# The first 128 queries of batch 0 mixed by selection matmuls instead of gathers

## The chip, the cores and the metric

One core of a Trainium2 chip runs the kernel. The metric is the device time of one execution in microseconds (us).

## The reference

Talking-heads attention, followed by a feed-forward layer with a squared ReLU. There are 8 batches, 12 heads, 448 tokens and a head width of 64; the feed-forward layer has 768 inputs, 2048 hidden units and 768 outputs.

```python
scores = scale * np.matmul(q, k.transpose(0, 1, 3, 2))
scores = np.einsum('bhij,hg->bgij', scores, w_pre)      # heads mixed before the softmax
attn = softmax(scores)                                  # over j
attn = np.einsum('bhij,hg->bgij', attn, w_post)         # heads mixed after it
x = np.matmul(attn, v)                                  # tokens x 768
h = np.maximum(x @ w_in, 0.0)
return h * h @ w_out
```

## The kernel before

The order of the instructions on PE and POOL is written out by hand; the other engines follow the order that the framework makes of the program. Each engine works through its list in order and waits on semaphores.

**Transposes.** `turn_unit` (L182, L186) transposes four heads of q and k of a batch on PE (`tr_ps`); ACT and DVE copy the results into `qT` and `kT`. For batch 0 the loads of q and k come first, in thirds, on POOL's DMA queue.

**Scores.** `score_pair` (L329, L333) computes the scores of two heads for 128 queries into two PSUM banks (`s_ps`). ACT copies one bank and DVE the other into a score block `S`, which has the queries on its 128 partitions and the heads along the free dimension. Six pairs fill a block; there are three block buffers. The next block may go into a buffer only when the readers of the old one have finished.

**Gathers.** The mix over heads is a matmul whose contracted dimension has to hold the heads. `gather` (L357) therefore copies the scores of 10 queries and 12 heads by DMA from `S` into a tile `G` with 120 rows (105 KB), in two halves of 60 rows, mostly on SP's queue. There are 8 such tiles, and 6 more at first, which lie in the last weight buffer (`w2_3`, shown as `w`) until the weights need it.

**Mix.** One turn of the main loop (`ds`, 180 turns) takes two query tiles of 10 queries. `mix` (L367) multiplies both with the 60x60 matrix `pre`, a block pattern of `w_pre`, in four matmuls of 64x64; the result is in two PSUM banks (`m_ps`). ACT takes the exponential and the row sums (L372), DVE the reciprocal (`rc`, L374), and POOL multiplies and subtracts the mean (`d`, L376).

**Unmix.** Two turns later `unmix` (L399) multiplies `d` with `post` into `at_ps`, and DVE copies that (L404) into the attention buffer `at`. `av_unit` (L199, L210) multiplies `at` with v, a third of a batch at a time. `ffn1_unit` (L251, L258, L260) and `ffn2_unit` (L281) are cut into small pieces and used as filler between turns.

**Loads.** Loads of the weights, of v and of later batches are put on POOL's queue at fixed turns (`at_load`). A load stands in line with POOL's arithmetic, so it is issued only when POOL gets there.

**Spins.** `spin` (L429) issues 16 matmuls on the identity whose results nobody uses, once before the loop and in each of turns 0 to 9.

PSUM has eight banks, which all of `tr_ps`, `s_ps`, `m_ps`, `at_ps`, `ot_ps`, `h_ps`, `o_ps` and the spins take in rotation.

Of the kernel before, what the change touches and what calls it, by code (L numbers as in the profile page):

```python
# [9 lines left out]
BF16 = mybir.dt.bfloat16  # L10
F32 = mybir.dt.float32
ACT = mybir.ActivationFunctionType
ALU = mybir.AluOpType
PE, POOL = mybir.EngineType.PE, mybir.EngineType.Pool

B, H, S, D = 8, 12, 448, 64
# [7 lines left out]
IQ = 10  # L24
# [7 lines left out]
AHEAD = 6  # L32
LEAD = 14
MORE = 6
HEAD = 3 * (AHEAD + 2 + MORE)
OFF = 64 - H * (IQ // 2)
SCALE = 1.0 / 8.0
FIRST_TURN = (13, 14, 15)
# [6 lines left out]
def kernel(  # L45
# [46 lines left out]
    def wcol(w, name, eng, p0s):  # L92
# [4 lines left out]
            eng.dma_start(out=t[p0:p0 + HR, 0:H], in_=src)  # L97
        return t

    col_pre = wcol(w_pre, "col_pre", nc.sync, (OFF, 64))  # L100
    col_post = wcol(w_post, "col_post", nc.scalar, (0, 64))

# [25 lines left out]
    for t in dts:  # L128
        nc.vector.memset(t[:, S:DW], 0.0)

    shared = wts.tile([P, FT // 4 * DMODEL], BF16, name="w2_3", tag="w2_3", bufs=1)
    gts = [work.tile([P, S], BF16, name=f"G{x}") for x in range(AHEAD + 2)]
    more = [shared[:, S * x:S * x + S] for x in range(MORE)]
    for t in gts + more:
        nc.vector.memset(t[0:OFF, :], 0.0)

    def gather_tile(n):
        if n < HEAD:
            n = n % (AHEAD + 2 + MORE)
            return more[n - AHEAD - 2] if n >= AHEAD + 2 else gts[n]  # L140
        return gts[(n - HEAD) % (AHEAD + 2)]

    def gather_end(ds):
        return min(2 * ds + AHEAD + 2 + MORE, max(HEAD + AHEAD + 2, 2 * ds + AHEAD + 2))

    attn = [atp.tile([P, VS, H, TW], BF16, name=f"at{x}") for x in range(2)]
    for t in attn:
# [3 lines left out]
    cgblk = consts.tile([P, NPAIR], F32, name="cgblk")  # L151
    wpost_bf = consts.tile([H, H], BF16, name="wpost_bf")
    w1 = [wts.tile([P, NPAIR, DFF // 4], BF16, name=f"w1_{x}") for x in range(4)]
    w2 = [wts.tile([P, FT // 4, DMODEL], BF16, name=f"w2_{x}") for x in range(3)]

    qTs, kTs, bvecs, xts, h2ts, ats = {}, {}, {}, {}, {}, {}

# [30 lines left out]
    def av_unit(b, part, cp):  # L188
        at = ats[(b, part)]
        first = part == 0  # L190
        q0 = IQ * PARTS[b % 2][part]
        n = min(IQ * PARTS[b % 2][part + 1], S) - q0
        c0 = 0 if first else 2
        ps = bank("ot_ps")
        for y in range(3):
            for r in range(VS):
                for hh in range(2):
                    g = 6 * cp + 2 * y + hh
                    nc.tensor.matmul(ps[64 * hh:64 * hh + 64, TW * y + c0:TW * y + 2 + n], lhsT=vs[b][:, g, r, :],  # L199
                                     rhs=at[:, r, g, c0:2 + n], start=(y == 0 and r == 0), stop=(r == VS - 1),  # L200
                                     skip_group_check=True)
        if b not in xts:
            xts[b] = ffnp.tile([P, NPAIR, S], BF16, name="xt", tag="xt", bufs=2)
            bvecs[b] = [work.tile([P, 3], F32, name="bvec", tag="bvec", bufs=4) for _ in range(2)]
        bv = bvecs[b][cp]
        if first:
            nc.vector.tensor_tensor(out=bv[:, :], in0=ps[:, 0:3 * TW].rearrange("p (y t) -> p y t", t=TW)[:, :, 1],
                                    in1=cgblk[:, 3 * cp:3 * cp + 3], op=ALU.mult)
        for y in range(3):
            nc.scalar.activation(out=xts[b][:, 3 * cp + y, q0:q0 + n], in_=ps[:, TW * y + 2:TW * y + 2 + n],  # L210
                                 func=ACT.Identity, bias=bv[:, y:y + 1], scale=1.0)
# [24 lines left out]
    def load_w2(x):  # L236
        n = DFF // 8
        c = x % 2 * 2
        if x == 6:
            last = wts.tile([P, FT // 4 * DMODEL], BF16, name="w2_3", tag="w2_3", bufs=1)  # L240
            w2.append(last[:, :].rearrange("p (c m) -> p c m", m=DMODEL))
        nc.gpsimd.dma_start(out=w2[x // 2][:, c:c + 2, :],
                            in_=moe_w_out[n * x:n * x + n, :].rearrange("(c p) m -> p c m", p=P))

# [87 lines left out]
        for hh, copy in enumerate((nc.scalar.copy, nc.vector.tensor_copy)):  # L332
            copy(out=Sb[n][z0:z1, 2 * p + hh, :], in_=pss[hh][z0:z1, 0:S])  # L333

    def queries(t, y):
        return max(0, min(HQ, S - IQ * t - HQ * y))

    def span_of(s):
        b, t = s
        c = IQ * t  # L340
        return half_of(b, c) // 2, half_of(b, min(c + IQ, S) - 1) // 2

    def needs(s):
# [1 line left out]

    def gather(k):

        b, t = steps[k]
        c, end = IQ * t, min(IQ * t + IQ, S)
        g = gather_tile(k)  # L350
        eng = nc.scalar if k in (1, 3) else nc.sync
        row = OFF
        while c < end:
            n, z = divmod(half_of(b, c), 2)
            x = PR * z + c % PR
            m = min(end - c, P - x)
            eng.dma_start(out=g[row:row + H * m, :], in_=Sb[n][x:x + m, :, :])  # L357
            c, row = c + m, row + H * m
        Gs[k] = g

    def mix(k):
        pss = [bank("m_ps") for _ in range(2)]
        gs = [Gs.pop(2 * k + x) for x in range(2)]
        for y in range(2):
            for x in range(2):
                rows = slice(64 * y, 64 * y + H * queries(steps[2 * k + x][1], y) if y else 64)
                nc.tensor.matmul(pss[y][64 * x:64 * x + 64, 0:S], lhsT=pre[rows, :], rhs=gs[x][rows, :],  # L367
                                 start=True, stop=True)
        for y in range(2):
            e = work.tile([P, S], F32, name="e_sb", tag="E", bufs=3)  # L370
            sm = work.tile([P, 1], F32, name="sm", tag="sm", bufs=4)
            nc.scalar.activation(out=e[:, :], in_=pss[y][:, 0:S], func=ACT.Exp, scale=SCALE, accum_out=sm[:, 0:1])  # L372
            rc = work.tile([P, 1], F32, name="rc", tag="rc", bufs=4)
            nc.vector.reciprocal(out=rc[:, :], in_=sm[:, :])  # L374
            d = dts[(2 * k + y) % ND]
            nc.gpsimd.tensor_scalar(out=d[:, 0:S], in0=e[:, :], scalar1=rc[:, 0:1], scalar2=-1.0 / S,  # L376
                                    op0=ALU.mult, op1=ALU.add)
            dsb[(k, y)] = d

    def place_of(s):  # L380
        b, t = s
        part = sum(t >= x for x in PARTS[b % 2]) - 1
        if (b, part) not in ats:
            ats[(b, part)] = attn[(3 * b + part) % 2]
        return ats[(b, part)], 2 + IQ * (t - PARTS[b % 2][part])

    def unmix(k):

        places = [place_of(s) for s in steps[2 * k:2 * k + 2]]
        us = [bank("at_ps") for _ in range(2)]  # L390
        for y in range(2):
            d = dsb.pop((k, y))
            for r in range(VS):
                c = HR * (VS * y + r)
                for x in range(2):
                    rows = slice(64 * x, 64 * x + HR)
                    for z in range(2):
                        j = PR * (r + (R - VS) * z) if r or not z else S
                        nc.tensor.matmul(us[x][PR * z:PR * z + PR, c:c + HR], lhsT=d[rows, j:j + PR],  # L399
                                         rhs=post[rows, :], start=True, stop=True)  # L400
        for x, (at, c) in enumerate(places):
            src = us[x][:, 0:2 * VS * HR].rearrange("p (y m i) -> p m y i", y=2, i=HQ)
            dst = at[:, :, :, c:c + IQ].rearrange("p r g (y i) -> p (r g) y i", y=2)
            nc.vector.tensor_copy(out=dst, in_=src)  # L404

# [27 lines left out]
    with tc.manual_schedule(engines={PE, POOL}):  # L433
# [9 lines left out]
        def at_load(i, f, *args):  # L443
            loads.setdefault(i, []).append(lambda: f(*args))
# [1 line left out]
        for x in range(2):  # L446
            at_load(-1, load_w1, x)
        for x in range(4):
            at_load(-1 if x < 2 else 2, load_v, 0, x)
            at_load(44 + 2 * x, load_v, 1, x)  # L450
        for x in range(2, 8):
            at_load(1 + x, load_w1, x)
        for x in range(6):
            at_load(11 + 2 * x, load_qk, 1, x)
            at_load(52 + 2 * x, load_qk, 2, x)
# [2 lines left out]
        for b in range(1, B):  # L458
            if b + 2 < B:
                for x in range(6):  # L460
                    at_load(NT * b + 34 + 2 * x, load_qk, b + 2, x)
            if b + 1 < B:
                for x in range(4):
                    at_load(NT * b + 46 + 2 * x, load_v, b + 1, x)
        nd = len(steps) // 2
        issued, gathered = [NPAIR + 3], [0]
        spans = [span_of(s) for s in steps]
# [9 lines left out]

        def scores_for(ds, most):
            want = math.ceil(place(gather_end(ds) + LEAD - 2))
            full = sum(gathered[0] >= x for x in lasts)  # L480
            want = min(want, issued[0] + most, NPAIR * min(full + 3, blocks))
            want = max(want, needs(steps[min(2 * ds + 4, len(steps) - 1)]))
            while issued[0] < want and all(issued[0] % NPAIR < turned.get(x[1], 0) for x in halves(issued[0] // NPAIR)):
# [10 lines left out]
        gathers_for(-1)  # L494
        for n in range(NPAIR, issued[0]):
            score_pair(n)
        spin(4)
        for f in loads.get(-1, []):
            f()
        for ds in range(nd + LAG):  # L500
            for i in (2 * ds, 2 * ds + 1):
                for f in loads.get(i, []):
# [19 lines left out]
            if old2:  # L522
                unmix(ds - LAG)
                for b1, t1 in old2:
                    ends = PARTS[b1 % 2]
                    if t1 + 1 in ends:
# [1 line left out]
                        for x, u in enumerate(av_units(b1, part)):  # L528
                            at_step(ds + (2 + x if b1 else 1), u)
                        if b1 == 0:  # L530
                            c = (IQ * ends[part], min(IQ * ends[part + 1], S))
                            at_step(ds + 1, (0, lambda c=c: filler.extend(ffn1_units(0, *c))))
                    if t1 == NT - 1:
                        if b1 > 0:
# [8 lines left out]
            if now2:  # L543
                mix(ds)
            gathers_for(ds)
            if ds < PARTS[0][1] // 2 + LAG:
                spin(4)
            if ds + 1 < nd + LAG:
                fill(share)
# [39 lines left out]
```

The softmax here doesn't subtract the row's maximum and nothing guards it: scores larger than these inputs give would overflow.

## Time and profile before

| What | Value |
|---|---|
| Median of 13 runs | 588.53 us (583.49 to 593.37) |
| The profiled execution | 587.95 us, with a span of 586.2 us |
| Mean granted PE clock | 0.982 |
| PE busy | 542.4 us, 93% of the span |
| DVE, ACT, POOL busy | 408.0, 407.4, 399.4 us |
| First 60 us: PE busy | 36.21 us |
| Gathers in the chain that ended last | 4% of the span for `G<-S`, 3% for `w<-S` |

The span goes from the first to the last instruction of the profiled execution. The page divides it into forty slices of 14.65 us each. Busy shares are averages over stages with different limits, so tables by stage and the chain of waits matter more than the totals. "w" in the profile stands for several weight buffers: for `w1`, for `w2`, and for the six gather tiles that lie in `w2_3`.

### The profile page before, as it was taken

How to read it: one execution, taken by the hardware profiler on the slowest of the kernel's cores; microseconds unless marked ns; L12 is line 12 of the kernel's file. 1: busy time of each engine (PE TensorE's matmuls, PEld its weight loads, DVE VectorE, ACT ScalarE, POOL GpSimd, SP SyncE). 2: the span in 40 equal slices, each digit the busy share in tenths (PEclk: the TensorE clock that was granted, in tenths of full speed). 3: DMA queues.
4: the chain of work that ended last, by engine and by line, in shares of the span. 5: the costliest groups of instructions: out<-in, count | busy, mean ns of one | idle time of the engine just before them, and what ended most of it. 6: DMA issues, size and time to landing. Idle time of an engine off the chain costs nothing.

```text
span 586.2 us, 28172 instructions
## 1 busy us (share of the span) xinstructions
PE 542.4 (93%) x11810; PEld 309.3 (53%) x11810; DVE 408.0 (70%) x1050; ACT 407.4 (70%) x1223; POOL 399.4 (68%) x599
## 2 busy tenths in 40 slices
PE   2776997999899999999999999999999999999997
PEld 1443765655455555545655556545545555555554
DVE  5767786889777787677777787778777778756001
ACT  3756786878588767896688767886688768863320
POOL 5466578847667965897678865897578666782540
PEclk9979799999899999999999999999999999999999
DMA  9899879858963698448953697459943477442103
GB/s 136 142 217 178 186 152 162 160 103 156 196 137 75 109 192 169 93 87 146 206 115 73 117 199 149 90 89 173 192 101 75 83 153 145 85 79 57 41 14 82
DMA packets 83364, 74.98 MB, mean 128 GB/s; under 512 B 6436, under 2 KB 80164, under 8 KB 83236
## 3 DMA queue, kind: packets, MB, share of 16 engines
q1 hardware_dynamic: 51502, 49.26, 36.1%
q0 software_dynamic: 31264, 23.60, 29.8%
q8 instruction: 92, 1.51, 1.0%
q10 hardware_dynamic: 470, 0.32, 0.2%
q14 instruction: 36, 0.29, 0.1%
HBM read 47.20 MB, written 11.01 MB: 99 GB/s over the span
## 4 chain that ended last, share of the span: by engine, by line
PE 78%; DMA 7%; DVE 4%; ACT 3%; POOL 2%; issue 2%; ACTq 0%; DVEq 0%
PE o_ps L281 25%; PE h_ps L251 25%; PE at_ps L399 10%; PE ot_ps L199 7%; PE m_ps L367 6%; DMA G<-S 4%; PE s_ps L329 4%; DMA w<-S 3%; DVE at L404 2%; PE tr_ps L182 2%; ACT xt L210 2%; POOL d L376 1%; ACT e_sb L372 1%; POOL w L232 1%; DVE S L333 1%
## 5 line engine op out<-in xcount | busy, mean ns | idle before, releaser
L376 POOL TENSOR_SCALAR d<-e_sb,rc 128x448 bf16<-128x448 f32 x360 | 226.6, 640 | 146.9 <-DVE rc L374 145.5
L404 DVE CAST at<-at_ps 128x480 bf16<-128x480 f32 x360 | 220.0, 651 | 67.0 <-PE at_ps L399 60.2
L372 ACT ACTIVATE e_sb<-m_ps 128x448 f32<-128x448 f32 x360 | 195.7, 559 | 21.8 <-PE m_ps L367 16.8
L251 PE MATMUL h_ps<-xt,w 128*128 128x448 bf16 (+2 forms) x960 | 164.3, 320 | 1.7 <-DVE at L404 1.3
L281 PE MATMUL o_ps<-w,h 128*128 128x384 bf16 (+1 forms) x1024 | 163.1, 329 | 0.5 <-ACT xt L210 0.5
L260 POOL TENSOR_TENSOR h<-hr 128x448 bf16<-128x448 f32 (+2 forms) x136 | 113.7, 845 | 15.9 <-ACT hr L258 15.9
L251 PEld LDWEIGHTS <-w 128*128 128x128 bf16 x960 | 80.8, 99 | 78.3 <-issue 29.3
L281 PEld LDWEIGHTS <-h 128*128 128x128 bf16 (+1 forms) x1024 | 82.4, 101 | 71.9 <-issue 26.7
L333 ACT CAST S<-s_ps 128x448 bf16<-128x448 f32 (+1 forms) x174 | 90.8, 542 | 41.5 <-PE s_ps L329 40.7
L333 DVE CAST S<-s_ps 128x448 bf16<-128x448 f32 (+1 forms) x174 | 104.5, 614 | 0.4 <-PE s_ps L329 0.4
L399 PEld LDWEIGHTS <-d 60*64 60x64 bf16 x5760 | 64.1, 110 | 58.0 <-issue 35.7
L399 PE MATMUL at_ps<-post,d 60*64 60x60 bf16 x5760 | 84.8, 195 | 9.3 <-issue 3.8
L258 ACT ACTIVATE hr<-h_ps 128x448 f32<-128x448 f32 (+2 forms) x160 | 74.5, 487 | 19.5 <-PE h_ps L251 13.7
L374 DVE RECIPROCAL rc<-sm 128x1 f32<-128x1 f32 x360 | 53.0, 158 | 44.4 <-ACT e_sb L372 42.0
L367 PE MATMUL m_ps<-G,pre 64*64 64x448 bf16 (+2 forms) x684 | 73.9, 358 | 10.5 <-DMA G<-S 6.7
L372 ACT ACTIVATION_READ_ACCUMULATOR e_sb<-m_ps 128x1 f32 x360 | 78.8, 219 | 0.0
L210 ACT ACTIVATE xt<-ot_ps,bvec 128x160 bf16<-128x160 f32 (+3 forms) x144 | 44.7, 385 | 45.4 <-PE ot_ps L199 36.1
L329 PE MATMUL s_ps<-kT,qT 64*64 64x448 bf16 x672 | 64.2, 370 | 0.8 <-issue 0.3
L288 DVE COPY osb<-o_ps 128x384 f32<-128x384 f32 x48 | 26.0, 548 | 36.8 <-PE o_ps L281 36.6
L199 PE MATMUL ot_ps<-at,v 128*64 128x160 bf16 (+4 forms) x1152 | 45.9, 229 | 0.0
L199 PEld LDWEIGHTS <-v 128*64 128x64 bf16 x1152 | 38.4, 109 | 13.7 <-issue 12.3
L367 PEld LDWEIGHTS <-pre 64*64 64x64 bf16 x720 | 28.4, 107 | 30.0 <-issue 22.4
(42 smaller groups left out, 214.6 us busy)
## 6 DMA issues: line engine op xcount, KB each, us to landing
G<-S SPq DMA_DIRECT2D x314, 105.0 KB
out_dram<-osb SPq DMA_DIRECT2D x48, 192.0 KB
v<-in_v_dram POOLq DMA_DIRECT2D x32, 192.0 KB, 5.7
qkst<-in_k_dram POOLq DMA_DIRECT2D x24, 224.0 KB, 5.5
qkst<-in_q_dram POOLq DMA_DIRECT2D x24, 224.0 KB, 6.4
w<-in_moe_w_in_dram POOLq DMA_DIRECT2D x8, 384.0 KB, 10.6
w<-in_moe_w_out_dram POOLq DMA_DIRECT2D x8, 384.0 KB, 6.3
w<-S SPq DMA_DIRECT2D x15, 105.0 KB
```

The source lines that it names most:

```text
L199: nc.tensor.matmul(ps[64 * hh:64 * hh + 64, TW * y + c0:TW * y + 2 + n], lhsT=vs[b][:, g, r, :], rhs=at[:, r, g, c0:2 + n], start=(y == 0 ...
L251: nc.tensor.matmul(ps[:, 0:n], lhsT=w1[ft // 4][:, c2, ft % 4 * 128:ft % 4 * 128 + 128], rhs=xts[b][:, c2, c0:c1], start=(c2 == 0), stop=( ...
L258: nc.scalar.activation(out=hr[:, 0:n], in_=ps[:, 0:n], func=ACT.Relu)
L260: square.tensor_tensor(out=h2ts[(b, ft)][:, c0:c1], in0=hr[:, 0:n], in1=hr[:, 0:n], op=ALU.mult)
L281: nc.tensor.matmul(dst, lhsT=h2ts[(b, ft)][:, mt * 128:mt * 128 + ROWS[mt]], rhs=w2[ft // 4][:, ft % 4, n2 * 384:(n2 + 1) * 384], start=(f ...
L329: nc.tensor.matmul(pss[hh][PR * z:PR * z + PR, 0:S], lhsT=qTs[b][rs, p, PR * j:PR * j + PR], rhs=kTs[b][rs, p, :], start=True, stop=True)
L333: copy(out=Sb[n][z0:z1, 2 * p + hh, :], in_=pss[hh][z0:z1, 0:S])
L367: nc.tensor.matmul(pss[y][64 * x:64 * x + 64, 0:S], lhsT=pre[rows, :], rhs=gs[x][rows, :], start=True, stop=True)
L372: nc.scalar.activation(out=e[:, :], in_=pss[y][:, 0:S], func=ACT.Exp, scale=SCALE, accum_out=sm[:, 0:1])
L376: nc.gpsimd.tensor_scalar(out=d[:, 0:S], in0=e[:, :], scalar1=rc[:, 0:1], scalar2=-1.0 / S, op0=ALU.mult, op1=ALU.add)
L399: nc.tensor.matmul(us[x][PR * z:PR * z + PR, c:c + HR], lhsT=d[rows, j:j + PR], rhs=post[rows, :], start=True, stop=True)
L404: nc.vector.tensor_copy(out=dst, in_=src)
```

## The change

Thirteen tiles (`FIRST`) now cover the first 128 queries of batch 0, which are exactly score block 0. For these tiles there is no gather. Instead, `mix` multiplies the score block itself with weighted selection matrices. For each head h and each half of 64 queries, `zs` holds, for every query, a column for each output head with the weight `w_pre[h, g]` in the row of that query. Sixty-four such columns starting at the tile's first query, multiplied with the score block of head h and accumulated over the twelve heads, give the mixed scores of five queries. This is 48 matmuls of 64x64 for two tiles instead of four.

The matrices are built at the start from the identity and from a broadcast copy of `w_pre` (`wpre`, loaded on SP ahead of `col_pre`). DVE builds the parts for heads 0 to 7 in four products, POOL those for heads 8 to 11 in one. They lie in the buffers that later hold `w_out`. A tile now takes five queries from each half of the block, so `unmix` copies its result in two pieces. Tiles 13 to 44 of batch 0 take 10 queries each from query 128 on; the first third of batch 0 has 158 queries instead of 160.

The loads of v and `w_in` come earlier. All four loads of v of batch 0 and four of the eight of `w_in` are issued ahead of the loop and the other four at turns 0 to 3. The clearing of the six extra gather tiles moves from DVE to POOL in turns 0 to 2. The spin before the loop is gone, and the ones in the loop run in turns 6 to 9 alone. The gathers that ran on ACT's queue are gone; all gathers are on SP's queue.

```diff
+FIRST = 13
+FQ = 128
+ROUND = AHEAD + 2 + MORE
+HEAD = FIRST + 2 * ROUND
+ZH = 4
+ZW = 64 * H
...
+    wpre = shared[:, MORE * S:MORE * S + 2 * H * H].bitcast(F32)
+    nc.sync.dma_start(out=wpre,
+                      in_=bass.AP(tensor=w_pre.tensor, offset=w_pre[0, 0:1].offset, ap=[[0, P], [1, H * H]]))
...
-    for t in gts + more:
+
+    for t in gts:
         nc.vector.memset(t[0:OFF, :], 0.0)
...
+    zs = [wts.tile([P, ZH * ZW], BF16, name=f"w2_{x}", tag=f"w2_{x}", bufs=1) for x in range(3)]
+    idz = shared[:, MORE * S + 2 * H * H:MORE * S + 2 * H * H + 64]
+    nc.vector.tensor_tensor(out=idz, in0=ident[:, 0:64], in1=ident[:, 64:P], op=ALU.add)
+
+    def z_unit(x, eng, h0=0, h1=ZH):
+        eng.tensor_tensor(out=zs[x][:, ZW * h0:ZW * h1].rearrange("p (h q g) -> p h q g", h=h1 - h0, g=H),
+                          in0=idz.unsqueeze(1).unsqueeze(3).to_broadcast([P, h1 - h0, 64, H]),
+                          in1=wpre.rearrange("p (h g) -> p h g", g=H)[:, ZH * x + h0:ZH * x + h1, :].unsqueeze(2).to_broadcast([P, h1 - h0, 64, H]),
+                          op=ALU.mult)
+
+    for x in range(2):
+        for h in range(0, ZH, 2):
+            z_unit(x, nc.vector, h, h + 2)
...
     def gather(k):
 
+        if by_pe(k):
+            return
...
-        eng = nc.scalar if k in (1, 3) else nc.sync
+        eng = nc.sync
...
     def mix(k):
         pss = [bank("m_ps") for _ in range(2)]
-        gs = [Gs.pop(2 * k + x) for x in range(2)]
+        pair = (2 * k, 2 * k + 1)
+        gs = [None if by_pe(n) else Gs.pop(n) for n in pair]
+        for h in range(H):
+            for y in range(2):
+                rows = slice(64 * y, 64 * y + 64)
+                for x, n in enumerate(pair):
+                    if by_pe(n):
+                        c = ZW * (h % ZH) + H * query(0, n)
+                        m = min(64, ZH * ZW - c)
+                        nc.tensor.matmul(pss[y][64 * x:64 * x + m, 0:S], lhsT=zs[h // ZH][rows, c:c + m],
+                                         rhs=Sb[0][rows, h, :], start=(h == 0), stop=(h == H - 1),
+                                         skip_group_check=True)
...
+            if by_pe(2 * k + x):
+                for y in range(2):
+                    j = c + FQ // 2 * y
+                    nc.vector.tensor_copy(out=at[:, :, :, j:j + HQ].rearrange("p r g i -> p (r g) i"), in_=src[:, :, y, :])
+                continue
...
         for x in range(4):
-            at_load(-1 if x < 2 else 2, load_v, 0, x)
+            at_load(-2, load_v, 0, x)
             at_load(44 + 2 * x, load_v, 1, x)
         for x in range(2, 8):
-            at_load(1 + x, load_w1, x)
+            at_load(-2 if x < 4 else 2 * x - 8, load_w1, x)
...
+        for f in loads.get(-1, []):
+            f()
+        z_unit(2, nc.gpsimd)
+        for f in loads.get(-2, []):
+            f()
+        for x, t in enumerate(more):
+            at_load(x, nc.gpsimd.memset, t[0:OFF, :], 0.0)
...
-            full = sum(gathered[0] >= x for x in lasts)
+            full = sum(gathered[0] >= x for x in lasts) if 2 * ds >= FIRST else 0
...
-        spin(4)
-        for f in loads.get(-1, []):
-            f()
...
-            if ds < PARTS[0][1] // 2 + LAG:
+            if FIRST // 2 <= ds < PARTS[0][1] // 2 + LAG:
                 spin(4)
```

## The prediction

> **What bounds the kernel now.** I read first the page's forty slices, then the chain of waits, then tables by stage and the timeline of the first 100 us, because the edit touches only the first 128 queries.
>
> ```profile
> PE   2776997999899999999999999999999999999997
> DMA  9899879858963698448953697459943477442103
> 0.00:60.00 60.00, 36.21 (x906) 22.44 (x906) 38.30 (x114) 32.63 (x89) 34.91 (x60) 0.94 1.00 171
> 200.00:250.00 50.00, 49.20 (x1159) 27.75 (x1157) 37.15 (x96) 36.36 (x111) 34.77 (x53) 1.00 0.77 147
> 17.04 3.73 DMA G<-S
> 33.03 12.32 DMA G<-S
> 47.08 11.49 DMA w<-S
> 67.60 3.33 DMA w<-S
> ```
>
> The two stage rows give length, then busy time of PE, PEld, DVE, ACT and POOL, then clock, DMA share, GB/s. From 200 us on PE is busy 49.20 of 50 us: PE sets the end, its order is fixed by the program, so a delay or gain early moves the whole rest. In the first 60 us PE is idle for 23.8 us while the DMA engines are full (share 1.00), and the chain (start, length, cause) runs through gathers for 27.5 us of it. That is what the change attacks. A gain here counts one for one, up to the moment when PE becomes full, which I put at loop turn ds=13 (two query tiles a turn); its mix ends at 62.7 us in the timeline.
>
> ```profile
> 8.28 0.62 DVE L186 COPY kT<-tr_ps 128x896 bf16<-128x896 bf16 x1 [0.18 <-PE tr_ps L182]
> 14.74 3.80 DVE L333 CAST S<-s_ps 128x448 bf16<-128x448 f32 x7
> 16.98 1.78 PE L429 MATMUL spin_ps<-ident 64*64 64x448 bf16 x16
> 27.50 0.93 PE L429 MATMUL spin_ps<-ident 64*64 64x448 bf16 x16
> 20.81 0.59 PE L367 MATMUL m_ps<-G,pre 64*64 64x448 bf16 x4 [1.68 <-DMA G<-S]
> 56.38 1.25 POOL L376 TENSOR_SCALAR d<-e_sb,rc 128x448 bf16<-128x448 f32 x2
> 57.22 1.01 DVE L260 TENSOR_TENSOR h<-hr 128x160 bf16<-128x160 f32 x1
> 57.60 0.44 POOL L260 TENSOR_TENSOR h<-hr 128x160 bf16<-128x160 f32 x1
> ```
>
> Timeline rows (start, length): DVE is the first to be needed after the transposes, at 8.28, and its casts of scores decide when mixing may begin. PE's sixteen spin matmuls take 1.78 us early and 0.93 us later. DVE's 160-element product, 0.32 us at 61.45, took 1.01 us when POOL worked beside it.
>
> [...] the 1.01 us product began at 57.22, inside POOL's second d (ends 57.63), and ended at 58.23, after POOL's h (ends 58.04): it waited for both. [...] 16 matmuls in 0.93 us are a 0.36 us one plus three rounds of 0.19 us, so four run together. [...]
>
> **The change part by part.** The sum is made against the profiled run: span 586.2 us, time 587.95, so 1.75 us lie around the span. It is 0.6 below the median of 588.53; I add the difference to the median.
>
> A. *Building the selection weights.* The order of the changed program puts four DVE products of 128x1536 (zs 0 and 1) ahead of every kT copy, behind `post`, which waits for col_post until 7.87. No row shows this size; [...] They run from 8.3 to 15.2 if nothing blocks them. Behind them queue three kT copies (0.62 each) and the score casts (0.55 each); PE waits for both. By program order eleven score pairs precede mix(0), and with eight PSUM banks mix(0) needs the eighth cast: 15.2 + 3x0.62 + 8x0.55 = 21.5. Before, mix(0) was at 20.81. The gather of 3.73 us is saved, yet the start is +0.7. The w_pre broadcast on SP (74 KB) lands before 8 us and delays only col_pre, by one issue of 0.85 us, hidden by the wait for col_post. Removing six DVE memsets (1.45 us, L135) gains nothing, since DVE waits for col_post anyway.
>
> B. *The same product on POOL* (zs 2, 128x3072) becomes ready at 8.3 as well, when idz is done. POOL's h rows give (932-388)/320 = 1.70 ns an element, so 5.4 us; [...] I take 6.0. [...] Lower bound 0: DVE's four hold on one after another, POOL comes last, and mix(0) needs zs 2 only at head 8. [...] I take 6.0 for zs 2 plus 0.7 for one DMA issue: +6.7. POOL itself, with v and w1 behind zs 2, is free by about 22 and its first d is due after 26: no cost. The six memsets of 4x448 on POOL (a DVE one took 0.245) fit in the same slack, three turns at about 2.5 us of POOL work under a 2.7 us turn.
>
> C. *The mixes.* 48 matmuls for 4, in 12 rounds of 0.19: 2.4 us for 0.6, so +1.8 in turn 0. [...] I add 1.5 for half clock (bounds 0, and 2.2 when the whole mix is slow). M0, the end of mix(0), moves by 0.7+1.8+1.5 = +4.0. Turns 1 to 6 then: a turn allocates up to eight banks (two at, four scores, two m), so in turns 2 and 3 a mix must wait for the two exps of the turn before, 1.25 us: 2.7+3.6+3.6+3.0+2.8+1.8 = 17.5. Before, these six took 39.1-21.4 = 17.7. So -0.2: thirteen missing gathers are paid for in matmuls. DVE's by-half copies (four of about 0.4 for two of 0.61) give 3.1 us in those turns, under 3.6. The seven spin groups removed lay in idle PE time: 0.
>
> D. *Turns 7 to 13.* Gathers for tiles 13 to 26 start when the second score block is cast, at turn 1, and SP needs 0.88 for each issue: 14 are out 12.3 us later, before their mixes. So the DMA waits go, and DVE is late next: two rc 0.32, two copies 1.22, casts 0.61, some 0.1 between, 2.25 a turn; seven turns and one attention-times-V of 1.87 are 17.6. Before: 62.7-39.1 = 23.6. So -6.0 (bounds -3 with w1 and qk loads still crowding, -7). v and w1 issued earlier have landed by then; the qk loads, one a turn on POOL, are the new last arrival for the transposes of turn 13.
>
> E. *After turn 13.* PE is near full. Of the 3.33 us wait at 67.60 I take 0.7 as gained (0 to 3); the rest of the program is the same.
>
> Sum: +4.0 -0.2 -6.0 -0.7 = -2.9 without the exclusion of B; +6.7 with it: +3.8. On the median: 592.3.
>
> **Rivals.** *R1, no exclusion at the start* (DVE keeps its turn, or POOL's product slips behind): -2.9, 585.6, on the other side. For it: DVE's four instructions stand back to back, and the trace shows no such pair at this length. Against: 1.01 us at 57.22, where POOL's next instruction passed the waiting DVE. It decides at B: when the last zs product on DVE ends before about 18.1 us (15.2+2.9), the change wins. *R2, R1 with a larger relief*: less traffic also removes the 3.33 us wait and the PE gap at 97.13 (3.40 us, put down to "issue"): 588.5-2.9-2.6-3.4 = 579.6. For: 1.4 MB less in the full stage. Against: that gap comes 35 us later. *R3, half clock lasts*: the mixes stay slow through several turns [...]: 6.5 mixes at 4.5 instead of 2.25 us, less the 1.5 counted: +13 at most, half of it +6.5, so 598.8. For: clock 0.55 from 35 to 40 us in the trace[...].
>
> **How the numbers follow.** Forecast 0.55 (its own range 587.5 to 597), R1 0.23, R2 0.09, R3 0.13. A difference of 0.5% (2.9 us) is about what a measurement can tell from no change. Slower by more: 0.37 of the forecast's 0.55 and all of R3, 0.50. Faster: 0.03 of the forecast, half of R1 and R2 whole, 0.24. The rest, 0.26, within. The range leaves out half of R2 and the ends of R3: 582 to 598.
>
> **What would show it.** In the profile after: [...] the first kT copy near 22 us (15.2 in R1); first mix near 28, lasting 2.4 to 4.5; no DMA wait before tiles 13 to 26; mix of turn 13 ending near 67.2 (60.5 in R1). I am wrong if the four DVE products end by 16 us, or if the turns after 6 still wait for gathers.

## The result, and the profile after

The changed kernel takes 598.89 us (median of 11 runs, 594.94 to 602.34) against 587.54 (48 runs of the kernel before, made beside them). The ratio of the two is 1.0193, with a 95% interval of 1.0165 to 1.0222: 11.3 us slower. The prediction had 592.3 and a range up to 598. The profiled execution has a span of 598.9 us. Executions more than 1.5% above the fastest of their kernel are left out of the ratios below but not of the medians, and r9_spin16 was profiled in one of them, so its trace is used for positions only.

The slices of the page after (tenths of busy time, forty slices) and the row of the first stage (columns as before):

```profile
PE   1398789789999999999999999999999999999997
DMA  8878957985995389646974499548953477342103
```
```profile
0.00:60.00 60.00, 34.24 (x887) 23.23 (x891) 41.87 (x106) 24.46 (x63) 37.23 (x55) 0.97 0.83 137
```

In the first 60 us the DMA share falls from 1.00 to 0.83: the gathers of the first 13 tiles are gone. PE is nevertheless busy for 2.0 us less than before. A mix now takes 48 matmuls instead of 4, but PE gets less far in these 60 us (887 matmuls against 906). The first two slices show why (1 and 3, before 2 and 7): PE stands still at the start. The timeline of the start (start, length), with `post` of the kernel before as the first line:

```profile
7.87 0.22 DVE L118 TENSOR_TENSOR post<-stripe_post,col_post 128x60 bf16<-128x60 f32 x1 [1.27 <-DMA col_post<-in_w_post_dram]
```
```profile
11.35 0.22 DVE L127 TENSOR_TENSOR post<-stripe_post,col_post 128x60 bf16<-128x60 f32 x1 [0.63 <-DMA col_post<-in_w_post_dram]
11.70 11.95 DVE L182 TENSOR_TENSOR w<-w 128x1536 bf16<-128x1536 bf16 x4
11.76 6.94 POOL L182 TENSOR_TENSOR w<-w 128x3072 bf16<-128x3072 bf16 x1 [4.05 <-DVE w L179]
13.38 6.93 DVE L182 TENSOR_TENSOR w<-w 128x1536 bf16<-128x1536 bf16 x1
23.57 1.14 DVE L221 COPY kT<-tr_ps 128x896 bf16<-128x896 bf16 x2
29.56 2.89 PE L412 MATMUL m_ps<-S,w 64*64 64x448 bf16 x48
```

`post` waits for col_post until 11.35 (7.87 before). Then DVE's four products take 11.95 us together. One by one they take 1.76, 6.93, 1.75 and 1.75 us: the second (shown alone in the fourth line) ends at 20.31, 1.61 us after POOL's product (18.70). The kT copies and every score follow the products. The chain of waits (start, length, cause) has this start in it, and three later places:

```profile
2.36 8.86 DMA col_post<-in_w_post_dram
11.70 11.95 DVE w L182 x4
...
52.21 0.75 SPq L397
53.06 1.21 DMA G<-S
54.81 0.52 ACT S L368
...
71.98 3.38 issue
...
79.32 1.41 issue
```

To follow the delay through the program, I take from the traces the start of the second exp of a turn on ACT (us). "Control" is the changed kernel profiled once more (run r14_after_again).

| kernel | turn 0 | 6 | 13 | 16 | 40 | 179 | median |
|---|---|---|---|---|---|---|---|
| before | 21.9 | 40.2 | 63.7 | 72.0 | 138.3 | 532.9 | 587.54 |
| after | 32.8 | 50.9 | 70.8 | 85.4 | 151.9 | 545.4 | 598.89 |
| control | 33.0 | 53.9 | 70.5 | 79.8 | 146.6 | 541.7 | 597.05 |
| r5_one_head | 23.6 | 42.8 | 59.3 | 71.5 | 139.5 | 532.3 | 588.28 |
| r6_loads_before | 32.7 | 52.2 | 76.9 | 86.3 | 153.4 | 550.4 | 604.04 |
| r7_all | 25.1 | 43.6 | 60.0 | 71.7 | 141.0 | 534.9 | 589.88 |
| r10_all_w2_later | 24.3 | 43.4 | 60.5 | 69.3 | 137.9 | 532.5 | 589.33 |
| r11_all_spin8 | 24.1 | 42.6 | 59.4 | 69.5 | 137.0 | 531.5 | 589.22 |
| r13_all_spin8_w2 | 28.0 | 46.4 | 62.7 | 72.2 | 140.8 | 534.5 | 589.94 |

The rows are single executions, the medians are over the timed runs. From turn 40 to the end every row lasts 392.8 to 397.0 us (394.6 before), so what decides the kernel happens in the first quarter.

### The profile page after: what moved, and what is told of

Read it like the earlier page. It is cut to its first block, busy times and chain, and to the rows that moved or that the text cites. A ratio compares the mean times of both kernels' runs of the same rounds, so it can differ in the third digit from the quotient of the medians.

```text
span 598.9 us, 28505 instructions
## 1 busy us (share of the span) xinstructions
PE 547.3 (91%) x11984; PEld 315.3 (53%) x11984; DVE 419.4 (70%) x1062; ACT 407.2 (68%) x1223; POOL 408.5 (68%) x606
## 4 chain that ended last, share of the span: by engine, by line
PE 77%; DVE 7%; DMA 6%; ACT 5%; issue 3%; POOL 2%; ACTq 0%; SPq 0%; DVEq 0%; POOLq 0%
PE o_ps L316 24%; PE h_ps L286 23%; PE at_ps L452 9%; PE ot_ps L234 7%; PE m_ps L420 5%; PE s_ps L364 4%; DMA G<-S 3%; PE m_ps L412 3%; DVE at L462 2%; DVE w L182 2%; PE tr_ps L217 2%; ACT e_sb L425 2%; ACT xt L245 2%; DMA col_post<-in_w_post_dram 1%; POOL d L429 1%
## 5 line engine op out<-in xcount | busy, mean ns | idle before, releaser
L462 DVE CAST at<-at_ps 128x480 bf16<-128x480 f32 x347 | 212.1, 651 | 63.5 <-PE at_ps L452 55.0
L286 PE MATMUL h_ps<-xt,w 128*128 128x448 bf16 (+3 forms) x960 | 165.4, 320 | 5.8 <-issue 2.7
L295 POOL TENSOR_TENSOR h<-hr 128x448 bf16<-128x448 f32 (+3 forms) x136 | 113.6, 844 | 16.4 <-ACT hr L293 16.4
L286 PEld LDWEIGHTS <-w 128*128 128x128 bf16 x960 | 81.4, 99 | 81.8 <-issue 32.7
L452 PEld LDWEIGHTS <-d 60*64 60x64 bf16 x5760 | 64.1, 109 | 51.0 <-issue 32.5
L293 ACT ACTIVATE hr<-h_ps 128x448 f32<-128x448 f32 (+3 forms) x160 | 74.4, 485 | 20.9 <-PE h_ps L286 14.6
L420 PE MATMUL m_ps<-G,pre 60*64 60x448 bf16 (+2 forms) x670 | 73.3, 357 | 6.0 <-DMA G<-S 2.7
L245 ACT ACTIVATE xt<-ot_ps,bvec 128x160 bf16<-128x160 f32 (+5 forms) x144 | 44.7, 385 | 45.5 <-PE ot_ps L234 36.2
L234 PE MATMUL ot_ps<-at,v 128*64 128x160 bf16 (+5 forms) x1152 | 45.9, 229 | 0.0
L234 PEld LDWEIGHTS <-v 128*64 128x64 bf16 x1152 | 38.4, 109 | 13.5 <-issue 12.1
L420 PEld LDWEIGHTS <-pre 64*64 64x64 bf16 (+2 forms) x694 | 27.0, 107 | 19.0 <-issue 16.5
```

The costliest lines, as they stand in the source:

```text
L286: nc.tensor.matmul(ps[:, 0:n], lhsT=w1[ft // 4][:, c2, ft % 4 * 128:ft % 4 * 128 + 128], rhs=xts[b][:, c2, c0:c1], start=(c2 == 0), stop=( ...
L293: nc.scalar.activation(out=hr[:, 0:n], in_=ps[:, 0:n], func=ACT.Relu)
L295: square.tensor_tensor(out=h2ts[(b, ft)][:, c0:c1], in0=hr[:, 0:n], in1=hr[:, 0:n], op=ALU.mult)
```

## The experiments

The theory to be tested has three parts. The start costs about 11 us (building the matrices, and the late col_post). The relief in turns 7 to 13 is partly taken by a wait for a score block's buffer. What is left is taken by PE's idle stretches in turns 14 and 15, which the chain calls "issue". Rivals: the loads or the gathers bound these turns anyway; half clock carries the loss. With each result stands its ratio to the kernel before, run in the same group, and the 95% interval of that ratio. The kernel before had medians of 586.42 to 587.54 in these groups.

### The start: POOL's product, w_pre's place, nearly no matrices

r1_no_pool_product leaves POOL's product out:

```diff
-        z_unit(2, nc.gpsimd)
...
-lhsT=zs[h // ZH][rows, c:c + m]
+lhsT=zs[min(h // ZH, 1)][rows, c:c + m]
```

> POOL's product for heads 8 to 11 is left out; the mix reads the matrices of heads 4 to 7 again for these heads, so the values of the first 128 queries are wrong and only the time counts. Theory (the two products exclude each other): DVE's four products take 6.9 us instead of 11.95, the first kT copy and the first mix come 5 us earlier, and the end moves by about -5 us (594). Rival (the four are slow in themselves, or POOL's DMA issues hold DVE as well): they stay near 12 us and the time stays at 599.

Measured: 597.16 us, ratio 1.0165 [1.0133, 1.0197]. DVE's timeline:

```profile
11.82 6.76 DVE L182 TENSOR_TENSOR w<-w 128x1536 bf16<-128x1536 bf16 x4
18.50 1.15 DVE L221 COPY kT<-tr_ps 128x896 bf16<-128x896 bf16 x2
```

The four products take 6.76 instead of 11.95 us: POOL's one instruction costs DVE 5.19 us. The exp of turn 0 comes at 28.0, 4.8 earlier than in the changed kernel. So the mechanism of the theory is shown, but not its gain of 5 us: the median falls by 1.7 us only, and the intervals of the two ratios overlap. (The profiled execution, 594.44 us, was the fastest of the four.)

r2_wpre_behind issues the broadcast of w_pre later:

```diff
-    nc.sync.dma_start(out=wpre, ...)     # ahead of col_pre
...
     for t in gts:
         nc.vector.memset(t[0:OFF, :], 0.0)
+    nc.vector.memset(wpre, 0.0)
+    nc.sync.dma_start(out=wpre, ...)     # behind col_pre and col_post
```

> The broadcast load of w_pre goes out behind the two col_pre loads on SP instead of ahead of them; nothing else moves. Theory (128 rows of 576 bytes ahead of the small loads hold them up): col_pre and col_post land near 6.4 and 7.9 us as before the change, DVE's products start near 8.5 instead of 11.7, and the end moves by -3 us (596). Rival (the small loads are late for another reason, such as the loads of q and k): they land at 10.5 and 11.4 as now, no change; or the products now wait for w_pre itself, no change either.

Measured: 596.91 us, 1.0132 [1.0086, 1.0178]. The edit also clears wpre first, so the broadcast is issued at 3.39 us instead of 0.76. col_post is used at 7.45, but the products wait for w_pre itself until 9.96:

```profile
9.96 8.61 DVE L183 TENSOR_TENSOR w<-w 128x1536 bf16<-128x1536 bf16 x2 [2.19 <-DMA w<-in_w_pre_dram]
```

The exp of turn 0 is at 31.2, 1.6 earlier. In the profiles with the broadcast ahead of the columns `post` runs at 10.85 to 14.1; with it behind, at 6.97 to 8.77 in five of six (11.81 in r13). So the late column goes with the early broadcast. How one delays the other is not shown. col_post goes out on ACT's queue, not on SP's. The last packet of the broadcast ends at 3.55 us, that of col_post at 10.92, and in between (3.6 to 11 us) the packets of POOL's queue take 99.2% of the time of the 16 engines. Moving the broadcast is worth little alone, since the next input is late too.

r5_one_head takes the building away nearly whole:

```diff
-    for x in range(2):
-        for h in range(0, ZH, 2):
-            z_unit(x, nc.vector, h, h + 2)
+    z_unit(0, nc.vector, 0, 2)
...
-        z_unit(2, nc.gpsimd)
...
-c = ZW * (h % ZH) + H * query(0, n)
-m = min(64, ZH * ZW - c)
+c = H * query(0, n)
+m = min(64, 2 * ZW - c)
...
-lhsT=zs[h // ZH][rows, c:c + m]
+lhsT=zs[0][rows, c:c + m]
```

> The changed kernel with one product of 128x1536 on DVE in place of four, and none on POOL; every head's mix reads the matrices of the first head group, so the output of the first 128 queries is computed with the weights of the wrong heads; the instructions of the mixes, their number and their tiles stay. It takes nearly the whole of steps A and B away and leaves C, D and E. Theory (the building of the matrices sets the start, and PE is full later): the first exp falls from 32.8 us to about 23, near the 21.9 of before, and the time falls by most of these 10 us, to 588 to 591. Rival (what is gained at the start meets the gathers and loads, whose pace DMA sets, and PE's waits in turns 7 to 16 grow by as much): first exp near 23 all the same, but the time at 593 to 597, with the delay against before growing from about 1 us in turn 0 to 7 or more by turn 16.

Measured: 588.28 us, 1.0020 [0.9993, 1.0047].

```profile
11.62 1.76 DVE L182 TENSOR_TENSOR w<-w 128x1536 bf16<-128x1536 bf16 x1
...
20.31 2.89 PE L410 MATMUL m_ps<-S,w 64*64 64x448 bf16 x48
```

The time falls by 10.6 us, so the products account for the size of the loss, even though `post` is as late here (11.27) as in the changed kernel. But part of what the rival foresaw is there too: at turn 13 this kernel is 4.4 us ahead of before (59.3 against 63.7), at turn 16 only 0.5. Mixing without gathers does gain; three turns give it back. That DMA's pace takes it, as the rival had it, this run does not show.

### The loads

r6_loads_before and r8_before_loads exchange the schedules of v and w_in:

```diff
# r6, on the changed kernel
-            at_load(-2, load_v, 0, x)
+            at_load(-2 if x < 2 else 2, load_v, 0, x)
...
-            at_load(-2 if x < 4 else 2 * x - 8, load_w1, x)
+            at_load(1 + x, load_w1, x)
# r8, on the kernel before
-            at_load(-1 if x < 2 else 2, load_v, 0, x)
+            at_load(-1, load_v, 0, x)
...
-            at_load(1 + x, load_w1, x)
+            at_load(-1 if x < 4 else 2 * x - 8, load_w1, x)
```

> The changed kernel with the load schedule of before for v and w_in (two v loads and two w_in loads at the start, the others one turn after the other), all else as in the changed kernel. Theory (PE's idle stretches in turns 14 and 15 come from its instruction fetch waiting behind loads, whichever loads they are; w_out's are the ones there): they stay, 597 to 600. Rival (the loads that run on without a pause are what fills the DMA queues at the wrong time): 592 to 595, with turns 13 to 16 back near the 8.3 us of before from the 14.6 of the changed kernel.

> The kernel before with the load schedule of the changed kernel (v and the first w_in loads at the start without a pause), and its gathers as they were. Theory (the load schedule is nearly neutral; the matrices and what follows from them cost the time): 586 to 590. Rival (the loads in a row delay gathers or the instruction fetch and cost several us by themselves): 592 or more.

Measured: r6 604.04 us, 1.0267 [1.0201, 1.0334]; r8 586.48 us, 0.9974 [0.9950, 0.9998]. Both expectations of r6's time missed: the old schedule is not better but worse. (Its turns 13 to 16 took 9.4 us, near what the rival said, but the control, with no edit at all, took 9.3.) r6's timeline at turn 7:

```profile
59.69 0.95 ACT L368 CAST S<-s_ps 64x448 bf16<-64x448 f32 x2 [6.85 <-DMA w<-S]
60.27 1.71 PE L487 MATMUL spin_ps<-ident 64*64 64x448 bf16 x16 [6.70 <-ACT S L368]
```

A cast of a score waits 6.85 us for gathers, and PE behind it 6.70. SP issues the gathers at nearly the same times as in the changed kernel (from 33.8 and 33.9 us on), but with loads spread over the first turns they land later: the chain waits from 37.53 to 59.55 for them. So the part of the change that lets the loads run on does what it should; by itself it is worth 0.26% on the kernel before, with an interval that only just excludes no change.

### Turn 7: the buffer of the fourth score block

In the changed kernel the same cast waits:

```profile
54.38 0.95 ACT L368 CAST S<-s_ps 64x448 bf16<-64x448 f32 x2 [2.81 <-DMA G<-S]
54.96 0.95 PE L487 MATMUL spin_ps<-ident 64*64 64x448 bf16 x16 [2.80 <-ACT S L368]
```

The fourth score block needs one of the three score buffers. No gather reads block 0 in this kernel, and PE has mixed it by then. So a cast that waits for gathers is not going into the buffer of block 0: the pool has given it that of a block which the gathers are still reading (block 1, with its thirteen gathers, is the next oldest).

r3_slots gives every third block the same buffer:

```diff
-            Sb[n] = work.tile([P, H, S], BF16, name="S", tag="S", bufs=3)
+            Sb[n] = work.tile([P, H, S], BF16, name="S", tag=f"S{n % 3}", bufs=1)
```

> Score blocks go into three fixed buffers in turn, so the fourth block takes the place of block 0, which no gather reads, instead of block 1. Theory (the first cast of the fourth block waits for the thirteen gathers of block 1): the wait of 2.8 us of ACT at 51.4 goes, turn 8's mix comes 2.4 us earlier, the end moves by about -2.4 us (596.5). Rival (later turns are bound by the order of DVE and the transposes and give it back): less than 1 us.

Measured: 595.05 us, 1.0127 [1.0094, 1.0159], as the theory had it, and the only one of the single repairs whose interval lies below that of the changed kernel. From the exp of turn 6 to that of turn 7 it takes 2.0 us instead of 4.8, although `post` was as late as 12.68 in that profile. Without this edit the step is not always long: it took 2.0 us in r5 and 2.2 in the control.

### Everything at once

r7_all puts the repairs together: the slots of r3, w_pre behind as in r2, nothing on POOL, and the products in another form:

```diff
+    idz12, wpb = shared[:, 0:ZW], shared[:, ZW:ZW + H * H]
+    nc.vector.tensor_copy(out=idz12.rearrange("p (q g) -> p q g", g=H), in_=idz.unsqueeze(2).to_broadcast([P, 64, H]))
...
+    nc.vector.tensor_copy(out=wpb, in_=wpre)
...
+        nc.vector.tensor_tensor(out=zs[x][:, :].rearrange("p (h q g) -> p h q g", h=ZH, g=H),
+                                in0=idz12.rearrange("p (q g) -> p q g", g=H).unsqueeze(1).to_broadcast([P, ZH, 64, H]),
+                                in1=wpb.rearrange("p (h g) -> p h g", g=H)[:, ZH * x:ZH * x + ZH, :].unsqueeze(2).to_broadcast([P, ZH, 64, H]),
+                                op=ALU.mult)
```

> The changed kernel with all of the repairs at once: the three products on DVE alone in bf16 (inputs first copied to bf16, with the innermost run contiguous), none on POOL, the w_pre broadcast behind col_pre on SP, and score block n in buffer n modulo 3. Theory (A, B and the score block's slot explain most of the 11 us): the products take 1.6 to 3.2 us each and end by 16 to 21 us instead of 23.65; first exp at 24 to 29; no wait of the fourth score block for gathers in turn 7; time 588 to 592, about as before. If PE's waits for its instruction stream and for loads in turns 13 to 16 take the place of what is gained: 593 to 596.

Measured: 589.88 us, 1.0022 [0.9994, 1.0050], within what its theory had.

```profile
10.84 5.10 DVE L188 TENSOR_TENSOR w<-w 128x3072 bf16<-128x3072 bf16 x3
```

All three matrices are ready at 15.94 us, turn 7 no longer waits (2.0 us), and turn 13 comes 3.7 us ahead of before. At turn 16 the lead is 0.3. As in r5, the rest of the loss sits in turns 14 to 16.

### Turns 14 and 15: the "issue" stretches of PE

PE's timeline of the changed kernel:

```profile
69.79 0.99 PE L286 MATMUL h_ps<-xt,w 128*128 128x158 bf16 x12
...
71.56 0.42 PE L217 MATMUL tr_ps<-ident,qkst 64*64 64x64 bf16 x29
75.36 0.58 PE L217 MATMUL tr_ps<-ident,qkst 64*64 64x64 bf16 x27 [3.38 <-issue]
...
76.25 1.76 PE L286 MATMUL h_ps<-xt,w 128*128 128x158 bf16 x12
```

PE stops in the middle of 56 transposes, and the profile shows nothing that the rest of them waits for. The next h_ps group then runs at little over half speed (1.76 against 0.99 us; the granted clock from 76.0 to 78.2 us is 0.50). Counting matmuls in the trace, the stretches of 3.38, 1.41 and 2.69 us lie ahead of numbers 1245, 1373 and 2013, whole multiples of 128 apart. The trace also has packets of 16 KB on a DMA queue of their own (q8, kind "instruction"), one for about 128 matmuls with their weight loads (93 for 11984 on the page). One of them lies in or just ahead of each of these stretches: the first starts at 72.96, 0.98 us after PE has stopped, and takes 0.95 us. DMA queues of the changed kernel from 71 to 76 us (packets, MB, share of 16 engines):

```profile
q0 software_dynamic: 360, 0.52, 66.4%
q8 instruction: 1, 0.02, 1.2%
```

The traces of all runs together make this much stronger. They have 74 "issue" stretches of PE longer than 0.7 us, the first hundred matmuls left out. In every one PE goes on 1.2 to 1.8 us after the end of a 16 KB packet, and every one lies at a remainder of 82 to 95 modulo 128 (62 of them at 92 to 95; the remainder drifts down slowly through the program).

r4_w2_later moves the w_out loads, the ones under way there:

```diff
-            at_load(22 + 3 * x + (4 if x > 5 else 0), load_w2, x)
+            at_load(31 + 3 * x - (5 if x > 5 else 0), load_w2, x)
```

> The first six loads of w_out go out nine loop steps (4.5 turns) later. Theory (the PE gaps of 3.38 us at 72.0 and 1.41 us at 79.3 are instruction fetches that wait behind these loads): the gaps in turns 14 and 15 go, the end moves by -4 to -5 us (594.5). Rival (the gaps are waits for the transposes' own data, or fetches that are late at every 128th matmul whatever the loads): the gaps stay, 599; second rival: they move with the loads to later turns, 599.

Measured: 599.50 us, 1.0191 [1.0155, 1.0227]: no gain. The two stretches are still there, with 0.91 and 1.06 us. Turns 13 to 16 take 8.6 us instead of 14.6, turns 16 to 40 then 70.4 instead of 66.5: partly given back. (`post` ran at 14.1 in this profile.) As the control below shows, turns 13 to 16 can be that short without the edit.

r9_spin16, r15_spin8 and r11_all_spin8 shift the work against the count:

```diff
         for x in range(4):
             if x < 3:
                 turn_unit(0, x, (nc.scalar.copy, nc.vector.tensor_copy))
+            if x == 1:
+                spin(16)        # r15 and r11: spin(8)
```

> The changed kernel with 64 spin matmuls more, put in PE's idle 9.7 us at the start (14.5 to 24.2), where they should cost nothing. In the changed kernel PE's idle stretches of 3.38, 1.41 and 2.69 us lie ahead of the matmuls number 1245, 1373 and 2013 of the trace. These numbers are whole multiples of 128 apart, and 128 matmuls with their weight loads are one 16 KB packet of the instruction queue. Theory (PE waits for its instruction stream): the stretches stay at about the same numbers modulo 128 (1245, 1373, 2013), 64 matmuls earlier in the work, or vanish. Rival (PE waits for data or a semaphore of the work there): they move with the work to 1309, 1437 and 2077. Time 596 to 601 by both; down to 594 if the stretches vanish at the new place.

> The changed kernel with 32 spin matmuls in PE's idle 9.7 us at the start. Theory (borders of the instruction packets): an idle stretch stays at matmul 1245 and the one at 1373 shrinks below 1 us, as with the same shift in r11_all_spin8; turns 13 to 16 take 11 to 13 us instead of 14.6; 595 to 598. Rival (the shift by 64 matmuls cost time [...]): 601 or more.

> The changed kernel as it is, as a control beside the next run: 597 to 601 us, idle stretches of PE ahead of matmuls 1245 and 1373, more than 3 us together. If these stretches are not a property of the program but of one execution, they are elsewhere or absent, and their sum is below 2 us.

> r7_all with 32 spin matmuls more in PE's idle time ahead of the first scores. If the place of the instruction packets' borders in the work decides how long PE waits for them, the idle stretches of turns 14 and 15 (1.90 and 2.16 us, ahead of matmuls 1245 and 1373) stay at these numbers, 32 matmuls earlier in the work, and their lengths change; the time moves by up to 3 us either way from 589.9. If data is what PE waits for: the same stretches at 1277 and 1405, and 589 to 591.

Measured: r9 606.20 us, 1.0275 [1.0189, 1.0362]; r15 600.43 us, 1.0206 [1.0145, 1.0268]; the control r14 597.05 us, 1.0204 [1.0163, 1.0245]; r11 589.22 us, 1.0056 [1.0023, 1.0090]. PE in r15, with the work 32 matmuls later in the count:

```profile
69.64 0.72 PE L452 MATMUL at_ps<-post,d 60*64 60x60 bf16 x29
73.99 0.26 PE L452 MATMUL at_ps<-post,d 60*64 60x60 bf16 x3 [3.62 <-issue]
...
77.30 0.35 PE L217 MATMUL tr_ps<-ident,qkst 64*64 64x64 bf16 x21
79.09 0.47 PE L217 MATMUL tr_ps<-ident,qkst 64*64 64x64 bf16 x35 [1.44 <-issue]
```

The stretches stay at 1245 and 1373, and the first now cuts a group of at_ps instead of transposes. r9, with a shift of 64, has them at 1245 and 1373 too, where they cut a group of h_ps and one of at_ps; r11 has them there with 2.06 and 0.84 us. So PE waits for its instruction stream there, not for data: this is shown. What a shift is worth isn't: r15's expected gain did not come, and r9's interval is wide and reaches down to the changed kernel's. The control shows how much is the execution's own:

```profile
71.31 0.42 PE L217 MATMUL tr_ps<-ident,qkst 64*64 64x64 bf16 x29
72.48 0.41 PE L217 MATMUL tr_ps<-ident,qkst 64*64 64x64 bf16 x27 [0.76 <-issue]
...
75.94 0.22 PE L217 MATMUL tr_ps<-ident,qkst 64*64 64x64 bf16 x3 [1.06 <-issue]
```

The same two places, 0.76 and 1.06 us: below the 2 us that its rival named. Another such wait of 2.30 us had come in turn 6 (ahead of matmul 607), where r12 has one of 2.58. The place is the program's; the length changes from one execution to the next.

The lengths matter. In the fourteen profiles of the changed kernel and its variants (r9 left out), the time from turn 13 to turn 16 goes with the sum of the "issue" time of PE in it (correlation 0.91). It is 8.6 to 9.4 us where the sum is 2.0 us or less (r4, r6, the control), 13.5 and 14.6 us where it is about 5 (r15 and the changed kernel).

r10, r12 and r13 try to keep the lead on top of r7: r10 with r4's edit, r13 with r4's and r11's, r12 with each of the first six w_out loads in two halves:

```diff
-            at_load(22 + 3 * x + (4 if x > 5 else 0), load_w2, x)
+            if x > 5:
+                at_load(26 + 3 * x, load_w2, x)
+            else:
+                at_load(22 + 3 * x, load_w2, x, (0,))
+                at_load(24 + 3 * x, load_w2, x, (1,))
```

> The kernel with all repairs (run r7_all) and the first six w_out loads nine loop steps later. In r7_all turn 13 ends 3.7 us ahead of before (second exp at 60.0 against 63.7) and turn 16 level with it (71.7 against 72.0). Theory (w_out's loads make the instruction packets late in turns 14 and 15): turns 13 to 16 take 8.3 to 9 us, the lead stays, and the time is 584 to 587. Rival (the lead is given back wherever the loads are put, since the DMA engines have the same bytes to move by the first use of w_out at about 117 us): turns 13 to 16 quicker all the same, loss of 3 us or more between turns 20 and 40, time 588 to 592.

> r7_all with each of the first six w_out loads (384 KB) cut into two of 192 KB, a loop turn apart; the same bytes at nearly the same time. Theory (an instruction packet is late by the burst ahead of it): the idle stretches of turns 14 and 15, 4.06 us together, shrink to about half, time 586 to 588. Rival (it is late by the mean traffic of loads and gathers, or by a packet fetched too close ahead of its use, not by the burst): they stay within 1 us of 4, time 589 to 591.

> r7_all with both edits that shortened turns 13 to 16: 32 spin matmuls ahead of the first scores, and the first six w_out loads nine loop steps later. Theory (late instruction packets in turns 14 and 15 are what takes the lead of 3.7 us): both idle stretches gone, second exp of turn 16 at 68 to 69.5 against 72.0 in before, time 583.5 to 586. Rival (PE is not the only limit between turns 16 and 40; the lead is lost there to loads that come later): turn 16 at 68 to 69.5 all the same, 587 to 590.

Measured: r10 589.33 us, 1.0018 [0.9991, 1.0045]; r12 589.93 us, 1.0046 [1.0019, 1.0072]; r13 589.94 us, 1.0059 [1.0033, 1.0086]. In all three the rival fits the time better. r10 keeps 2.7 us of its 3.2 us lead at turn 16, and 0.4 at turn 40. r12's two stretches shrink to one of 2.30 us, but turn 6 has lost 2.58 at matmul 607. r13's start was late (`post` at 11.81, turn 0 at 28.0), so that its turn 16 is level with before; its turns 13 to 16 took 9.5 us, with stretches of 1.65 and 1.11 us still there. No version of the changed kernel beats the kernel before.

Why an instruction packet comes late in one execution and in time in another stays open. The DMA share (the number before the last) from turn 13 to turn 16 does not decide it. These are the rows of before, r7 and r10:

```profile
63.70:72.00 8.30, 7.96 (x274) 6.14 (x275) 6.76 (x18) 7.16 (x24) 6.49 (x11) 0.85 0.79 178
60.00:71.70 11.70, 7.45 (x261) 5.33 (x259) 7.44 (x19) 7.07 (x24) 7.41 (x13) 0.88 0.97 177
60.50:69.30 8.80, 6.50 (x240) 4.84 (x231) 6.75 (x18) 6.87 (x23) 5.88 (x10) 1.00 0.57 95
```

Before has no such stretch at a share of 0.79, the changed kernel 4.8 us of them at the same share, the control 1.8 at 0.91, r7 4.1 at 0.97, and r10 still 2.1 at 0.57. Neither moving nor halving the w_out loads removes the loss for good.

## Why the prediction was wrong, step by step

**A, B and C were right in sum, not in their terms.** They gave +10.7 us at the end of the first mix (4.0 plus 6.7) and +10.5 after turn 6; the traces show +10.9 (32.8 against 21.9) and +10.7. In A col_post was 3.5 us later than assumed: "delays only col_pre, by one issue of 0.85 us" is the sentence that failed. The stretch from 8.3 to 15.2 for the four products (6.9 us) was the author's estimate, on no row of before; without POOL's product they take 6.76 us (r1). B's exclusion, for which before has a single DVE product (1.01 us beside POOL, 0.32 alone), came: the second product took 6.93 us beside POOL's, the others 1.75 or 1.76. It cost 5.2 us (11.95 less 6.76), not 6.7. POOL's record is 6.94 us long, yet DVE's first product fills its beginning (to 13.46); the 5.24 us left are near the 5.4 that the prediction worked out from the h rows and then, by the author's estimate, raised to 6.0. The 0.7 for a DMA issue of POOL did not come: beside these issues, from 18.65 us on, DVE's last two products took 1.75 us each. In C half clock, the author's estimate too, added at most 0.5 us to the first mix (2.89 against 2.4, with a granted clock of 1.00 from 29.5 to 32.5 us), not 1.5. That these errors cancelled was luck. The six turns after took 18.1 us against 18.3 before, the -0.2 that was predicted. The control needed 20.9 us for them: an "issue" stretch of 2.30 us fell into its turn 6.

**D was mis-sized: -3.6 instead of -6.0.** From the exp of turn 6 to that of turn 13 it takes 19.9 us (23.5 before). The step asked what is late next in DVE, and missed that a score block needs a buffer that the gathers still read: 2.80 us of PE. Where the slot is fixed (r3, r7), it takes 16.4 to 16.5 us, that is about -7, at the far bound. In the control the step from turn 6 to turn 7 took 2.2 us, probably since turn 6 had already lost 2.30, and the seven turns took 16.6; but the delay at turn 13 was the same (6.8 against 7.1 us, 4.5 predicted). "No DMA wait before tiles 13 to 26" held for the mixes; the wait had moved to a cast of scores. The mix of turn 13 ended at 69.86 instead of 67.2.

**E had the wrong sign: -0.7 expected; from turn 13 to the last exp the delay grew by 5.4 us in the profile and by 2.0 in the control.** The step took "the rest of the program is the same" for granted. Instruction packets that came late made PE stand for 3.38 and 1.41 us in turns 14 and 15, and in the profile the granted clock from turn 13 to 16 was 0.65 (0.85 before). The kernel before has such a wait as well, the 3.40 us that the prediction knew as "issue":

```profile
100.54 0.26 PE L399 MATMUL at_ps<-post,d 60*64 60x60 bf16 x2 [3.40 <-issue]
```

It lies ahead of matmul 1884 with a 16 KB packet in it, and its remainder modulo 128 (92) is that of 1245 (93) within a record. The stretch of 2.69 us at 109.05 of the changed kernel stands against it and is no loss of its own; the stretches of turns 14 and 15 came on top. This is not one bad execution: in all fourteen profiles the delay grows from turn 13 to the end, by 0.7 to 5.7 us (median 2.9).

**The rivals.** R1's premise falls by the 11.95 us. But r5 and r7 make it true, with the last product on DVE ending at 13.38 and 15.94 us, before the 18.1 at which the prediction let the change win, and they take 588.28 and 589.88, not 585.6: step E would have failed there too. R2 falls: a 2.69 us "issue" stretch remains at 109.05. R3 named 598.8, within 0.1 us of the median, by luck: the six full mixes last 2.46 to 2.98 us, not 4.5, and the clock of the first 60 us is 0.97. That the spin groups taken out were worth nothing, as C had it, no run tests by itself. The change does what it says: the DMA share fell and no mix of the first 13 tiles waits for a gather.

## What to carry to other kernels

Removing gathers from a waiting stage pays only as far as what replaces them is ready in time: here 10 us of preparation on DVE and POOL ahead of the first copy cost about what the change lost. Before crediting a stage with relief, check which buffer its next producer is given and who still reads it, and in which place the program allocates it. Where PE shows "issue" gaps, count matmuls: here the gaps at a fixed remainder modulo 128 were the instruction stream, and a gain ahead of them vanished there (r5, r7) without any data being late. Before naming a cause from one profile, take a second one of the same kernel: the same two gaps had 4.79 us in one and 1.82 in the other.

## What the runs showed that had not been expected

- PE's instruction stream came as DMA packets of 16 KB, one per about 128 matmuls with weight loads (93 for 11984 in the changed kernel). It held PE at their borders for up to 3.62 us in the changed kernel's variants (r15) and 4.07 us in r8 (ahead of matmul 990). After the stretch of 3.38 us PE ran at little over half speed (12 h_ps matmuls 1.76 against 0.99 us, granted clock 0.50); after those of the control, 0.76 and 1.06 us, it did not (0.99).
- Three DVE products of bf16 inputs with contiguous inner runs of 12 took 5.10 us together, with 3072 columns each (r7); the changed kernel's form (fp32 second input, broadcast inner run) took 1.76 us for 1536 (r5). Which of the two differences does it was not tried.
- A column DMA of 2.8 KB took 8.86 us in the chain when a 72 KB broadcast was issued ahead of it, and was used 3.5 us later than before (11.35 against 7.87), although the broadcast itself was over at 3.55 us.
